# A linear-attention stage and a feed-forward stage: two programs in turn, laid out anew as one list schedule

## The chip, the cores and the metric

One core of a Trainium2 chip. The metric is the device time of one launch in microseconds; the inputs lie in device memory as float32, and the output goes back there as float32.

## What is computed

Four batches, eight heads, 768 steps, head size 48. The state of a head is a 48 x 48 matrix that decays row by row with w; the output of all heads, 384 numbers per token, goes through a multiplicative feed-forward part of 3072 tokens and width 1024.

```python
state = np.zeros((B, H, D, D))
for t in range(S):
    kt, vt, rt, wt = (k[:, :, t], v[:, :, t], r[:, :, t], w[:, :, t])
    cur = np.einsum('bhd,bhe->bhde', u[None] * kt, vt)
    y[:, :, t] = np.einsum('bhd,bhde->bhe', rt, state + cur)
    state = wt[:, :, :, None] * state + np.einsum('bhd,bhe->bhde', kt, vt)
x = y.transpose(0, 2, 1, 3).reshape(B * S, H * D)
h = (x @ w1) * (x @ w2) @ w3
out = h @ w_out
```

## The kernel before

The recurrence is done in chunks of 128 steps. Within a chunk, cumulative sums of log w (a matmul with a triangle of ones, `LT_incl` and `LT_strict`, L129 and L132) give the factors exp(-sum) for k and exp(sum) for r; a masked product of the two, times v, gives the part from inside the chunk, r times the state that the chunk began with gives the rest, and the state is carried on by k'v and the chunk's total decay (`pc_all`, L139).

Four things happen one after the other. First all constants and the four weights are set up; the weights go out on POOL's queue ahead of anything else (L84 to L87), cast to bfloat16 on the way. Then, two batches at a time (`bg`), a batch's whole r, k and v are loaded on POOL's queue (L113 to L115, pieces of 48 numbers, 6144 of them per load) and w on SP's (L116). For each batch a preparation runs over all its six chunks: the logarithm (L119), the sums, the exponentials (L130, L133), the scaled k and r (`Kt`, `Rt`, L131, L134), and the diagonal term r.(u k) v (L143 to L149). After it the chunks go by in order, the two batches in turn (L159): eight transposes of k, a copy from PSUM (`trsb`), eight of r, a copy (L166 to L171); eight products of r with the state (L178); the scores of four heads, mask, product with v, twice (L184 to L191); y goes to memory in bfloat16 (L196); eight products k'v and three small steps for the new state (L202 to L208). A head has 48 partitions in all of these.

When all of y is in memory, three transposing loads bring it back with the model dimension on partitions (L216). The feed-forward part goes by blocks of 512 tokens: eight times three matmuls each for a and b (L225, L228), ACT copies a, DVE multiplies by b (L232, L233); 64 matmuls with w3 (L239) and eight copies (L242); 32 with w_out (L247), four copies (L251) and four stores (L252).

The order on every engine is the program order. A tile framework puts the semaphores in and rotates the buffers of each pool.

Of the kernel before, what the change touches and what calls it, by code (L numbers as in the profile page):

```python
# [14 lines left out]
def kernel(
# [14 lines left out]

# [27 lines left out]
    LT_strict = consts.tile([C, C], BF)
    nc.gpsimd.memset(LT_strict, 1.0)
    nc.gpsimd.affine_select(LT_strict, LT_strict, compare_op=Alu.is_gt, fill=0.0,  # L60
                            base=0, channel_multiplier=-1, pattern=[[1, C]])

    mask_tiled = consts.tile([C, H, C], BF)
    nc.gpsimd.memset(mask_tiled, 1.0)
    nc.gpsimd.affine_select(mask_tiled, mask_tiled, compare_op=Alu.is_gt, fill=0.0,
                            base=0, channel_multiplier=-1, pattern=[[0, H], [1, C]])

    ones_c = consts.tile([C, 1], BF)
    nc.gpsimd.memset(ones_c, 1.0)

    I128 = consts.tile([C, C], BF)
    nc.gpsimd.memset(I128, 0.0)
    nc.gpsimd.affine_select(I128, I128, compare_op=Alu.not_equal, fill=1.0,
                            base=0, channel_multiplier=1, pattern=[[-1, C]])

    u_bc = consts.tile([C, H, D], F32)
    nc.sync.dma_start(u_bc, u.partition_broadcast(C))

    wpool = ctx.enter_context(tc.tile_pool(name="moe_w", bufs=1))
    w1_bf = wpool.tile([P, DI, DFF], BF)  # L80
    w2_bf = wpool.tile([P, DI, DFF], BF)
# [201 lines left out]
```

## Time and profile before

| | us |
|---|---|
| median of 3 runs (lowest, highest) | 418.54 (418.28, 418.82) |
| span of the profiled execution | 417.6 |
| PE busy | 315.4 |
| DVE busy | 175.6 |
| ACT busy | 154.9 |
| POOL busy | 33.4 |

The profile is of one execution, and it states its span, from the first to the last instruction; its whole time is not stated apart. The median of the runs is 0.9 us above that span, so the profiled execution is taken as one of them, and 0.9 us lie around the span. PE is TensorE, DVE VectorE, ACT ScalarE, POOL GpSimd, SP the queue that issues transfers. Busy PE time is pipelined and counts a matmul from its first to its last cycle, so matmuls overlap in it. The granted clock is given as a share of 2.4 GHz; 0.5 is 1.2 GHz.

### The profile page before, as it was taken

Reading aid. Unit: us, or ns where it says so; the run is one execution under the profiler, and the core shown is the slowest. Engines: PE = TensorE matmul, PEld = TensorE weight load, DVE = VectorE, ACT = ScalarE, POOL = GpSimd, SP = SyncE. Lnnn points to the kernel's source line nnn. Section 1 sums busy time; section 2 is a strip of 40 time slices with the busy share of each in tenths; the row PEclk is TensorE's granted clock in tenths of the full one; section 3 lists DMA queues with packets and bytes.
Section 4 is the critical chain, followed back from the end, with each engine's and each line's share of the span. In section 5 each row is a group of like instructions: output and inputs, shape, how many; then the busy total and the mean of one; then the engine's idle time right before and its main releaser. Section 6 shows DMA issues by size and latency. Waiting matters only on the chain.

```text
span 417.6 us, 5433 instructions
## 1 busy us (share of the span) xinstructions
PE 315.4 (76%) x2256; PEld 177.6 (43%) x2256; DVE 175.6 (42%) x264; ACT 154.9 (37%) x232; POOL 33.4 (8%) x29
## 2 busy tenths in 40 slices
PE   0301034677999747399992699999999999999996
PEld 0201021445777614177771244544544445445443
DVE  1000069795656899975573140330420411402502
ACT  1503033777465336345540133243232332331431
POOL 9100043412000400000000000000000000000000
PEclk9999999985555555655555599999999999999999
DMA  8999999979300980000004700200200201101002
GB/s 157 225 227 215 164 108 129 90 49 111 44 19 26 93 44 2 0 30 21 20 28 98 149 0 2 75 0 2 76 2 0 76 2 38 39 0 57 21 0 75
DMA packets 99400, 26.23 MB, mean 63 GB/s; under 512 B 84144, under 2 KB 97584, under 8 KB 99376
## 3 DMA queue, kind: packets, MB, share of 16 engines
q0 software_dynamic: 76800, 11.54, 40.4%
q1 hardware_dynamic: 22576, 14.36, 13.7%
q8 instruction: 17, 0.28, 0.3%
q14 instruction: 7, 0.06, 0.0%
HBM read 27.98 MB, written 7.08 MB: 84 GB/s over the span
## 4 chain that ended last, share of the span: by engine, by line
PE 63%; DVE 12%; issue 12%; ACT 4%; DMA 4%; POOL 3%; SPq 2%; ACTq 0%; POOLq 0%
PE h_ps L239 20%; PE a_ps L225 8%; PE o_ps L247 7%; PE b_ps L228 7%; PE Mps L184 5%; PE ktrps L166 4%; PE rtrps L170 4%; PE Yps L191 3%; DVE y_diag L149 2%; DMA v_bf<-in_v_dram 2%; DVE d_all L147 2%; DVE uk L146 2%; SPq L216 2%; PE Yps L178 2%; DVE Rt_bf L134 1%
## 5 line engine op out<-in xcount | busy, mean ns | idle before, releaser
L239 PE MATMUL h_ps<-abT,w_bf 128*128 128x512 bf16 x384 | 83.9, 379 | 0.0
L225 PE MATMUL a_ps<-xT,w_bf 128*128 128x512 bf16 x144 | 56.4, 396 | 11.7 <-DMA xT<-y_dram 11.7
L239 PEld LDWEIGHTS <-w_bf 128*128 128x128 bf16 x384 | 37.6, 98 | 45.3
L228 PE MATMUL b_ps<-xT,w_bf 128*128 128x512 bf16 x144 | 56.0, 393 | 0.0
L232 ACT COPY a_sb<-a_ps 128x512 f32<-128x512 f32 x48 | 28.1, 586 | 73.6 <-PE a_ps L225 72.2
L251 DVE COPY o_sb<-o_ps 128x384 f32<-128x384 f32 x24 | 13.4, 557 | 97.5 <-PE o_ps L247 97.5
L233 DVE TENSOR_TENSOR abT<-a_sb,b_ps 128x512 bf16<-128x512 f32 x48 | 33.0, 688 | 47.8 <-ACT a_sb L232 45.9
L242 ACT CAST hT<-h_ps 128x512 bf16<-128x512 f32 x48 | 28.1, 586 | 56.0 <-PE h_ps L239 56.0
L166 PE MATMUL ktrps<-I,Kt_bf 128*48 128x128 bf16 x192 | 30.3, 300 | 23.2 <-DVE Kt_bf L131 22.8
L167 ACT COPY trsb<-ktrps 48x1024 bf16<-48x1024 bf16 x24 | 24.1, 1005 | 38.4 <-PE Yps L178 36.9
L134 DVE TENSOR_TENSOR Rt_bf<-r_bf,Et 128x384 bf16<-128x384 bf16 x24 | 13.1, 546 | 54.9 <-DMA r_bf<-in_r_dram 50.8
L166 PEld LDWEIGHTS <-Kt_bf 128*48 128x48 bf16 x192 | 18.0, 139 | 33.9 <-DVE Kt_bf L131 23.0
L247 PE MATMUL o_ps<-wo_bf,hT 128*128 128x384 bf16 x192 | 32.2, 326 | 0.0
L186 DVE TENSOR_TENSOR Mbf<-Mps,mask_tiled 128x512 bf16<-128x512 f32 x48 | 30.7, 675 | 0.0
L170 PE MATMUL rtrps<-I,Rt_bf 128*48 128x128 bf16 x192 | 28.4, 304 | 2.3 <-ACT trsb L171 1.3
L129 PE MATMUL csp<-lw_bf,LT_incl 128*128 128x384 bf16 x24 | 11.0, 460 | 23.3 <-ACT lw_bf L119 12.8
L184 PE MATMUL Mps<-trsb 48*128 48x128 bf16 x192 | 28.6, 303 | 0.0
L195 DVE TENSOR_TENSOR y_c<-Yps,y_diag 128x384 bf16<-128x384 f32 x24 | 13.4, 557 | 31.2 <-PE Yps L191 31.2
L225 PEld LDWEIGHTS <-w_bf 128*128 128x128 bf16 x144 | 14.6, 101 | 27.6 <-issue 12.1
L171 ACT COPY trsb<-rtrps 48x1024 bf16<-48x1024 bf16 x24 | 24.1, 1005 | 2.1 <-PE rtrps L170 2.1
L130 ACT ACTIVATE NEt<-csp 128x384 f32<-128x384 f32 x24 | 11.7, 489 | 35.0 <-DVE Kt_bf L131 29.0
L247 PEld LDWEIGHTS <-hT 128*128 128x128 bf16 x192 | 18.8, 98 | 13.1
(51 smaller groups left out, 313.8 us busy)
## 6 DMA issues: line engine op xcount, KB each, us to landing
out_dram<-o_sb SPq DMA_DIRECT2D x24, 192.0 KB, 1.9
r_bf<-in_r_dram POOLq DMA_DIRECT2D x4, 576.0 KB, 10.5
k_bf<-in_k_dram POOLq DMA_DIRECT2D x4, 576.0 KB, 8.8
...
w_bf<-in_moe_w_dram POOLq DMA_DIRECT2D x2, 768.0 KB, 12.3
wo_bf<-in_moe_w_out_dram POOLq DMA_DIRECT2D x1, 768.0 KB, 32.2
```

The costliest lines, as they stand in the source:

```text
L166: nc.tensor.transpose(ktrps[:, h, :], Kt4[:, h, c, :], I128)
L167: nc.scalar.copy(trsb[:, 0], ktrps)
L170: nc.tensor.transpose(rtrps[:, h, :], Rt4[:, h, c, :], I128)
L184: nc.tensor.matmul(Mps[:, hi * C:(hi + 1) * C], lhsT=KtT[:, h, :], rhs=RtT[:, h, :], start=(hi == 0), stop=(hi == H // 2 - 1))
L186: nc.vector.tensor_mul(Mbf[:, g * (H // 2):(g + 1) * (H // 2), :], Mps.rearrange("s (h t) -> s h t", h=H // 2), mask_tiled[:, :(H // 2), :])
L225: nc.tensor.matmul(a_ps, lhsT=w1_bf[:, di, fi * P:(fi + 1) * P], rhs=xT[:, di, tb * TB:(tb + 1) * TB], start=(di == 0), stop=(di == DI - 1))
L228: nc.tensor.matmul(b_ps, lhsT=w2_bf[:, di, fi * P:(fi + 1) * P], rhs=xT[:, di, tb * TB:(tb + 1) * TB], start=(di == 0), stop=(di == DI - 1))
L232: nc.scalar.copy(a_sb, a_ps)
L233: nc.vector.tensor_mul(abT[:, fi, :], a_sb, b_ps)
L239: nc.tensor.matmul(h_ps, lhsT=w3_bf[:, fi, gi * P:(gi + 1) * P], rhs=abT[:, fi, :], start=(fi == 0), stop=(fi == FI - 1))
L242: nc.scalar.copy(hT[:, gi, :], h_ps)
L247: nc.tensor.matmul(o_ps, lhsT=hT[:, gi, ts * P:(ts + 1) * P], rhs=wo_bf[:, gi, :], start=(gi == 0), stop=(gi == FI - 1))
```

## The change

The whole kernel body is replaced. Operations are no longer issued where they are written. Each is entered into a list with its engine, a duration, what it reads and writes, a key (`prio`) and, where it needs them, PSUM banks; `schedule` then plays the list against those durations, an engine at a time taking the ready operation with the smallest key, and the program is issued in that order. A key is 100 per unit plus a small number, plus a constant of its kind from `RANK`. On the chip the engines run their lists in order, with semaphores between them as before.

A unit is two batches of one chunk, all sixteen heads; there are twelve, and units 2n and 2n+1 are chunk n of all four batches, 512 tokens. Each unit loads its own pieces (2048 per tensor, three buffers, four for v), so nothing is prepared ahead for a whole batch. A block is the feed-forward part of such 512 tokens and depends on the two units alone. y goes through PE transposes and one copy into `xT`; it is not stored.

w3 @ w_out is formed once on the chip (`w34_block`): eight times eight transposes of w3, a copy, eight matmuls, a copy. A block then has no w3 step.

Heads are paired: each has 64 columns, 48 of them used and the rest zero, so a transpose turns two heads at once, and a pair's scores are two products on partitions 0 to 63 and 64 to 127. The state of a pair is a 96 x 96 product of which the two diagonal parts are used (`Sbd`). The exclusive sum goes: r is multiplied by 1/w first (`RW`) and by the inclusive factor then. ruk, dv and the two state products are made on POOL, which had only constants and issues before. The copies out of PSUM are of 768, 1024 and 2048 elements. Of the diff, the parts with the keys and the operations (the removed body is the function printed above; only the lines of its that have no counterpart are repeated):

```diff
@@ -27,229 +185,424 @@
...
-        for bg in range(B // BG):
...
-                    nc.sync.dma_start(
-                        y_dram[b * S + c * C: b * S + (c + 1) * C, :].rearrange("t (h e) -> t h e", h=H),
-                        y_c)
...
-            nc.sync.dma_start_transpose(xT[:, di, :], y_dram[:, di * P:(di + 1) * P])
...
-                    nc.tensor.matmul(h_ps, lhsT=w3_bf[:, fi, gi * P:(gi + 1) * P],
-                                     rhs=abT[:, fi, :],
-                                     start=(fi == 0), stop=(fi == FI - 1))
...
+RANK = {
+    "I": -514.6, "KRT": 192.9, "KRk": 141.3, "KRr": 32.3, "LT": 346.9, "M": -298.0, "S": 275.9, "Sbd": 218.0,
+    "T": 19.3, "a": 0.7, "a_sb": 30.9, "abT": 45.1, "b": 1.1, "cs": -292.1, "dg": 759.1, "dv": -593.8,
+    "e": -725.8, "iw": 315.4, "kin": 76.5, "kv": -112.1, "ln": 105.7, "m": -532.2, "mask": -702.5,
+    "ne": 35.0, "o": 585.9, "ones": 266.0, "osb": 287.5, "pads": 788.5, "pc": -715.7, "rin": 68.6,
+    "rk": 96.2, "ruk": -33.8, "rw": 700.7, "state": 148.5, "store": -729.5, "table": -999.7, "tr": -53.7,
...
+WEIGHTS_AT = {
+    "w1": 9.47, "w2": 28.57, "w3a": 0.47, "w3b": 1.91, "wo": 1.05,
+}
...
+        kind = name.rstrip("_0123456789")
+        o = Op(eng, dur, fn, tuple(r), tuple(w), prio + RANK.get(kind, 0.0), self.LAT[eng], dma, kind, len(self.ops))
...
+                best = None
+                for o in pool:
+                    if ready_at[o] > t or (best is not None and (o.prio, o.seq) >= (best.prio, best.seq)):
+                        continue
+                    if any(self.psum[k]["at"] is None and place(self.psum[k]) is None for k in o.tiles):
+                        continue
+                    best = o
...
+    NI, NS = 3, 2
+    rin, kin, vin = (many(n, [C, BH, D], BF, x) for n, x in ((NI, "rin"), (NI, "kin"), (NI + 1, "vin")))
...
+    op("POOL", 300, c_lt, w=["LT"], prio=-42, name="LT")
...
+        ap = ROW[src][p * NB:(p + 1) * NB, :, c * C:(c + 1) * C, :].rearrange("b h t d -> t (b h) d")
+        e = nc.gpsimd if eng == "POOL" else nc.sync
+        op(eng, dur, lambda: e.dma_start(dst, ap), w=[key], prio=prio, dma=BH * C * (0.8 if eng == "POOL" else 0.85))
...
+    def wload(dst, src, key, prio, nbytes):
+        op("POOL", 950, lambda: nc.gpsimd.dma_start(dst, src), w=[key], prio=prio, dma=nbytes / 381.0)
...
+        load("SP", win[i], f"win{i}", "w", t, pr, 60)
+        load("POOL", kin[i], f"kin{i}", "k", t, pr + 1, 1350)
+        load("POOL", rin[i], f"rin{i}", "r", t, pr + 2, 1350)
+        load("POOL", vin[j], f"vin{j}", "v", t, pr + 3, 1350)
...
+    def w34_block(fi):
+        pr = 250 + fi * 12
...
+                nc.tensor.transpose(o[:, gi, :], w3_bf[:, fi, gi * P:(gi + 1) * P], I128)
...
+                nc.tensor.matmul(o[:, :DM], lhsT=w3T[fi % 2][:, gi, :], rhs=wo_bf[:, gi, :],
...
+        pr = t * 100.0
...
+        op("ACT", act(BH * D), lambda: nc.scalar.activation(LW[:, :, :D], ww, Act.Ln),
...
+                nc.tensor.matmul(o[:, b, :DM], lhsT=LT, rhs=LW[:, b * H:(b + 1) * H, :D], start=True, stop=True)
...
+                                     lhsT=LW[:, b * H + 2 * q:b * H + 2 * q + 2, :].rearrange("t h d -> t (h d)"),
...
+        op("PE", mm(384, 384, *[1] * BH), cs, r=[f"lw{s}", "LT", "ones"], w=[CS], prio=pr)
...
+        op("ACT", act(BH * D), lambda: nc.scalar.activation(IW, LW[:, :, :D], Act.Exp, scale=-1.0),
...
+        op("DVE", dve(BH * D, 2), lambda: nc.vector.tensor_mul(RW, rr, IW), r=[f"iw{s}", kr], w=[f"rw{s}"], prio=pr + 1)
...
+            nc.scalar.activation(N_.rearrange("t (b h) d -> t b (h d)", b=NB), o[:, :, :DM], Act.Exp, scale=-1.0)
...
+        op("DVE", dve(BH * D, 2), lambda: nc.vector.tensor_mul(KRs[:, 0, :, :D], kk, N_),
...
+        op("DVE", dve(BH * D, 2), lambda: nc.vector.tensor_mul(KRs[:, 1, :, :D], RW, E_),
...
+        op("DVE", dve(BH * D, 2), lambda: nc.vector.tensor_mul(rk[s], rr, kk), r=[kr, kk_], w=[f"rk{s}"], prio=pr + 8)
...
+            nc.gpsimd.tensor_mul(ruk[s].rearrange("t (b h) d -> t b h d", b=NB),
...
+        op("POOL", pool(BH * D), ruk_, r=[f"rk{s}", "u"], w=[f"ruk{s}"], prio=pr + 8)
+        op("DVE", dve(BH * D), lambda: nc.vector.reduce_sum(dg[s], ruk[s], axis=AX.X), r=[f"ruk{s}"], w=[f"dg{s}"], prio=pr + 9)
+        op("POOL", pool(BH * D), lambda: nc.gpsimd.tensor_mul(dv[s], vv, dg[s][:, :, None].to_broadcast([C, BH, D])),
...
+                        nc.tensor.transpose(o[:, b, q, :], KRs[:, x, h:h + 2, :].rearrange("t h d -> t (h d)"), I128)
...
+            nc.scalar.copy(KRTs.rearrange("p x b q t -> p (x b q t)"), o)
...
+                        nc.tensor.matmul(o[:, e, q, :], lhsT=KRTs[a:a + PAD, 0, b, q, :],
+                                         rhs=KRTs[a:a + PAD, 1, b, q, :], start=True, stop=True)
+            op("PE", mm(*[128] * H), mmul, r=[f"KRT{s}"], w=[MM], prio=pr + 7 + b)
...
+                nc.vector.tensor_mul(Mbf[m].rearrange("s j q t -> s (j q t)"), o.rearrange("s j f -> s (j f)"),
+                                     mask.rearrange("s q t -> s (q t)"))
+            op("DVE", dve(1024), msk, r=[MM, "mask"], w=[f"M{m}"], prio=pr + 7 + b)
...
+                        nc.tensor.matmul(o[:, q * 2 * D:(q + 1) * 2 * D], lhsT=KRTs[:, 1, b, q, :],
+                                         rhs=Sbd[p][:, b, q, :], start=first, stop=False)
...
+                    nc.tensor.matmul(o[:, h * D:(h + 1) * D], lhsT=Mbf[m][:, h % 2, h // 2, :],
...
+                nc.vector.tensor_add(yb[n], banks[:, g.at(Y), :][:, :DM],
...
+                    nc.tensor.transpose(o[:, di, b * C:(b + 1) * C],
...
+            nc.scalar.copy(xT[blk % 2][:, :, p * NB * C:(p + 1) * NB * C], o[:, :DI, :])
...
+                                         lhsT=KRs[:, 0, h:h + 2, :].rearrange("t h d -> t (h d)"),
+                                         rhs=vv[:, h:h + 2, :].rearrange("t h d -> t (h d)"), start=True, stop=True)
+            op("PE", mm(*[96] * (NB * HP)), kvm, r=[f"KRk{s}", kv], w=[KV], prio=pr + 11)
...
+                nc.vector.tensor_add(Tst[p].rearrange("p b q e -> p b (q e)"), o[:, :, :DM],
...
+                    nc.gpsimd.tensor_mul(Sbd[p][a:a + D, :, :, e * D:(e + 1) * D].rearrange("p b q e -> p (b q) e"),
...
+            op("POOL", 2 * pool(384), sbd, r=[f"T{p}", f"pc{t % (2 * NP)}"], w=[f"Sbd{p}"], prio=pr + 13)
...
+                    nc.gpsimd.tensor_mul(Sst[p].rearrange("p b q e -> p (b q) e"),
...
+                op("POOL", pool(768), snew, r=[f"T{p}", f"pc{t % (2 * NP)}"], w=[f"S{p}"], prio=pr + 14)
...
+        pr = (n * NP + NP - 1 + 0.9) * 100.0
...
+                    nc.tensor.matmul(banks[:, g.at(A), :], lhsT=wt[:, di, fi * P:(fi + 1) * P], rhs=xT[x][:, di, :],
...
+            op("PE", mm(512, 512, 512), am, r=xs + ["w1", "w2"], w=[A], prio=pr + fi)
+            op("PE", mm(512, 512, 512), bm, r=xs + ["w2"], w=[Bk], prio=pr + fi + 0.5)
...
+                nc.scalar.copy(a_sb[sa], banks[:, g.at(A), :])
...
+                nc.vector.tensor_mul(abT[x][:, fi, :], a_sb[sa], banks[:, g.at(Bk), :])
+            op("DVE", dve(TB), abm, r=[Bk, f"a_sb{sa}"], w=[f"abT{x}_{fi}"], prio=pr + fi - 30)
...
+                    nc.tensor.matmul(banks[:, g.at(O), :][:, :DM], lhsT=abT[x][:, fi, tt * P:(tt + 1) * P],
+                                     rhs=w34[:, fi, :], start=(fi == 0), stop=(fi == FI - 1))
+            op("PE", mm(*[DM] * FI), om, r=[f"abT{x}_{fi}" for fi in range(FI)] + [f"w34_{fi}" for fi in range(FI)],
+               w=[O], prio=pr + 40 + tt)
...
+                (nc.scalar.copy if tt % 2 else nc.vector.tensor_copy)(osb[so], banks[:, g.at(O), :][:, :DM])
+            op("ACT" if tt % 2 else "DVE", 500, oev, r=[O], w=[f"osb{so}"], prio=pr + 10 + tt)
...
+                nc.sync.dma_start(out[row:row + C, :], osb[so])
...
+        w34_block(fi)
+    for t in range(NU):
+        loads(t)
+        unit(t)
+        if t % NP == NP - 1:
+            block(t // NP)
...
+    order = g.schedule({"f": 4, "q": 6})
+    with tc.manual_schedule():
+        for o in order:
+            o.fn()
...
```

## Rows read from the trace of the kernel before

**Rows 1.** Stretches: length, busy PE, PEld, DVE, ACT, POOL, granted clock, DMA share, GB/s.

```profile
0.00:53.20 53.20, 5.58 (x99) 4.38 (x99) 1.45 (x5) 10.65 (x10) 11.24 (x19) 1.00 1.43 196
53.20:222.00 168.80, 129.33 (x1293) 87.94 (x1293) 126.64 (x186) 87.48 (x125) 22.11 (x10) 0.62 0.75 50
...
237.40:417.60 180.20, 176.73 (x856) 84.15 (x855) 46.38 (x72) 56.26 (x96) 0.00 (x0) 0.99 0.08 27
```

**Rows 2.** The chain that ended last: start us, us, what.

```profile
11.88 41.32 issue
...
115.98 0.66 PE ktrps L166 x5
...
120.43 0.66 PE ktrps L166 x5
...
277.69 13.81 PE h_ps L239 x64
291.51 5.20 PE o_ps L247 x32
```

**Rows 3.** PE in order of time near 100 us: start, us.

```profile
100.20 0.33 PE L178 MATMUL Yps<-S_bf,trsb 48*128 48x48 bf16 x4
100.47 0.73 PE L170 MATMUL rtrps<-I,Rt_bf 128*48 128x128 bf16 x5
...
103.72 0.41 PE L166 MATMUL ktrps<-I,Kt_bf 128*48 128x128 bf16 x2
...
104.70 0.50 PE L178 MATMUL Yps<-S_bf,trsb 48*128 48x48 bf16 x8
```

**Rows 4.** Stretches around the clock's fall and rise, columns as in rows 1.

```profile
92.00:94.00 2.00, 1.79 (x27) 1.38 (x25) 1.92 (x4) 1.99 (x2) 1.65 (x1) 0.50 0.17 53
...
100.00:222.00 122.00, 103.13 (x1069) 72.53 (x1068) 89.83 (x144) 59.09 (x87) 4.42 (x2) 0.51 0.34 34
...
241.00:242.00 1.00, 1.00 (x5) 0.35 (x3) 0.00 (x0) 0.24 (x1) 0.00 (x0) 0.67 0.00 0
```

**Rows 5.** Groups of DVE and ACT by shape: busy us, mean ns, idle before, releaser.

```profile
L232 ACT COPY a_sb<-a_ps 128x512 f32<-128x512 f32 x48 | 28.1, 586 | 73.6 <-PE a_ps L225 72.2 <-DVE abT L233 1.4
L149 DVE TENSOR_TENSOR y_diag<-v_bf,d_all 128x2304 bf16<-128x2304 bf16 x4 | 10.2, 2548 | 0.0
L119 ACT ACTIVATE lw_bf<-w_f 128x2304 bf16<-128x2304 f32 x4 | 8.5, 2123 | 22.5 <-DMA w_f<-in_w_dram 22.5
```

**Rows 6.** DVE in order of time near 90 us: start, us.

```profile
89.58 0.56 DVE L131 TENSOR_TENSOR Kt_bf<-k_bf,NEt 128x384 bf16<-128x384 bf16 x1
90.05 0.68 DVE L186 TENSOR_TENSOR Mbf<-Mps,mask_tiled 128x512 bf16<-128x512 f32 x1
90.65 0.55 DVE L134 TENSOR_TENSOR Rt_bf<-r_bf,Et 128x384 bf16<-128x384 bf16 x1
```

**Rows 7.** POOL in order of time; an issue counts as its work.

```profile
1.44 0.28 POOL L60 TENSOR_SCALAR_AFFINE_SELECT LT_strict<-LT_strict 128x128 bf16<-128x128 bf16 x1
2.75 1.08 POOL L65 TENSOR_SCALAR_AFFINE_SELECT mask_tiled<-mask_tiled 128x1024 bf16<-128x1024 bf16 x1
4.91 0.77 POOL L85 DMA_DIRECT2D w_bf<-in_moe_w_dram  x1
6.58 0.88 POOL L87 DMA_DIRECT2D wo_bf<-in_moe_w_out_dram  x1
9.64 2.24 POOL L114 DMA_DIRECT2D k_bf<-in_k_dram  x1
62.10 2.22 POOL L114 DMA_DIRECT2D k_bf<-in_k_dram  x1 [3.35 <-issue]
```

**Rows 8.** DMA: GB/s in 60 to 100 us; issues, KB, us to landing.

```profile
GB/s 142 145 145 145 116 77 137 144 145 116 126 130 145 142 20 0 0 28 128 132 140 144 143 145 156 134 38 7 0 0 0 0 8 98 0 59 137 133 145 114
...
out_dram<-o_sb SPq DMA_DIRECT2D x24, 192.0 KB, 1.9
...
wo_bf<-in_moe_w_out_dram POOLq DMA_DIRECT2D x1, 768.0 KB, 32.2
```

More of the change, by code (lines that the diff above doesn't have):

```diff
@@ L33 @@
     NC = S // C
-    HC = H * NC
     DM = H * D
@@ L58 @@
[L58 to L81, printed above, removed]
@@ L210 @@
[L210 to L226 removed]
+    HP = H // 2
@@ new lines, with many @@
+    PAD = 64
+    NB = 2
+    NP = B // NB
+    NU = NC * NP
+    TB = NP * NB * C
+    BH = NB * H
+    sb = ctx.enter_context(tc.tile_pool(name="sb", bufs=1))
+    ps = ctx.enter_context(tc.tile_pool(name="ps", bufs=1, space=bass.MemoryType.PSUM))
+    def many(n, shape, dt, name):
+        return [sb.tile(shape, dt, name=f"{name}_{i}", tag=f"{name}_{i}") for i in range(n)]
+    banks = ps.tile([P, 8, 512], F32, name="banks")
+    NI, NS = 3, 2
+    rin, kin, vin = (many(n, [C, BH, D], BF, x) for n, x in ((NI, "rin"), (NI, "kin"), (NI + 1, "vin")))
@@ new lines, with mm, act, dve @@
+    op = g.op
+    def mm(*cols):
+        return sum(max(n / 2.4 + 2.5, 42.0) for n in cols)
+    def act(n):
+        return 175 + 0.835 * n
+    def dve(n, x=1):
+        return 90 + 1.05 * n / x
+    def pool(n):
+        return 200 + 2.1 * n
+    def c_first():
+        nc.scalar.preload_act_table_set("natural_log_exp_and_others")
+    op("ACT", 1300, c_first, w=["table"], prio=-10, name="table")
+    def c_lt():
+        nc.gpsimd.affine_select(LT, LT, compare_op=Alu.is_ge, fill=0.0, base=0,
+                                channel_multiplier=-1, pattern=[[1, C]])
@@ new lines, in c_pads, with c_state @@
+    def c_pads():
+        for x in lw:
+            nc.vector.memset(x[:, :, D:], 0.0)
+        for x in KR:
+            nc.vector.memset(x[:, :, :, D:], 0.0)
+    def c_state():
+        for x in Sbd + Sst:
+            nc.vector.memset(x, 0.0)
+    op("DVE", 400, c_ones, w=["ones", "LT", "I128"], prio=-10, name="ones")
+    op("POOL", 300, c_lt, w=["LT"], prio=-42, name="LT")
+    op("POOL", 300, c_id, w=["I128"], prio=-41, name="I128")
+    op("DVE", 1500, c_pads, w=[f"lw{i}" for i in range(NS)] + [f"KR{x}{i}" for i in range(NS) for x in "kr"],
+       prio=-9, name="pads")
@@ new lines, with load @@
+    op("DVE", 900, lambda: nc.vector.memset(mask, 1.0), w=["mask"], prio=-8, name="mask1")
+    op("DVE", 2500, c_state, w=[f"S{i}" for i in range(NP)] + [f"Sbd{i}" for i in range(NP)], prio=-7, name="state0")
+    op("POOL", 1100, c_mask, w=["mask"], prio=-40, name="mask")
+    op("SP", 60, lambda: nc.sync.dma_start(u_bc, u.partition_broadcast(C)), w=["u"], prio=-5.0, dma=600.0, name="u")
+    ROW = {"r": r, "k": k, "v": v, "w": w}
+    def load(eng, dst, key, src, t, prio, dur):
+        c, p = divmod(t, NP)
+        ap = ROW[src][p * NB:(p + 1) * NB, :, c * C:(c + 1) * C, :].rearrange("b h t d -> t (b h) d")
+        e = nc.gpsimd if eng == "POOL" else nc.sync
+        op(eng, dur, lambda: e.dma_start(dst, ap), w=[key], prio=prio, dma=BH * C * (0.8 if eng == "POOL" else 0.85))
@@ L244 @@
[L244 to L252 removed]
+            xs = [f"xT{x}_{p}" for p in range(NP)]
@@ L256 @@
+    for fi in range(FI):
+        w34_block(fi)
[8 more added lines that the diff above has]
+            o.fn()
 _INS = ['r', 'k', 'v', 'w', 'u', 'moe_w1', 'moe_w2', 'moe_w3', 'moe_w_out']
```

481 lines of the change are left out of this document (328 added, 153 removed).

## The prediction, before the change was run

> **What bounds the kernel now.** I read the busy time of every engine in stretches first. The kernel is two programs in turn [rows 1]: up to 53.2 us TensorE is busy for 5.6 us, from there to 222 us attention runs with its clock granted at 0.62 on the mean, 15 us pass in handing over through memory, and the feed-forward part takes 180 us with PE busy for 176.7 of them and no other engine for more than 57. Next the chain of waits in order of time [rows 2]. In the first stage nothing but loading stands in it: POOL holds v's issue for 41.3 us. In attention the pieces repeat every 4.45 us per chunk and batch. In the feed-forward part it is one engine alone: 64 matmuls of w3 in 13.81 us and 32 of w_out in 5.20, six times. So one third of the span has no PE work, one third is PE at half clock, and only the last is PE at its rate.
>
> **Prices on PE.** 13.81 us for 64 is 215.8 ns per 512 columns, 5.20 for 32 is 162.5 per 384 [rows 2]. In attention five 128-column matmuls take 0.73 us and two take 0.41, so one more costs 107 ns; eight of 48 columns take 0.50 and four 0.33, so one costs 41 [rows 3]. That is columns at 1.2 GHz, and the granted clock says so: it fell to 0.50 at 92 us [rows 4], stayed there while PE issued transposes and small products without pause, and rose between 241 and 242 us, four microseconds after products of 512 columns had begun. I take half those prices, 54 and 20 ns, at 2.4 GHz.
>
> **Feed-forward part.** (h w3) w_out becomes h (w3 w_out): 384 matmuls of 215.8 ns go, 82.9 us. In their place stand, once, 64 transposes (3.5 us) and 64 products of 384 columns (10.4). A block keeps 48 of 512 and 32 of 384 columns: 15.56 us, 93.3 for six. Together 107.2 us.
>
> **Attention.** A unit is two batches of one chunk. One cumulative sum in place of two: 2 x 162 ns; 8 decay columns at 41 (0.33 us); 16 transposes of head pairs in place of 32, 0.87; 16 score products on 64 rows each. Whether two of these on different halves of the array run beside each other no row shows: between 0.43 and 0.86 us, and I take 0.86, the price of the same product before. Then 16 products of 48 and 8 of 96 columns, 0.66; 6 transposes of y, 0.33; 8 state products, 0.34. The sum is 3.7 us at full clock and 7.0 at half. Twelve units, less what the first and the last chunk leave out, are 43.1 us. The y store and the transposing loads, the 15 us of [rows 1], go altogether. **PE in all: 150.3 us**, where the feed-forward part alone had 180 us of its stretch.
>
> **The other engines.** DVE launches follow each other by 0.47 us for 384 and 0.60 for 512 elements, 0.07 more than one element per 0.96 GHz cycle [rows 6]. So 768 cost 0.87, 1024 cost 1.14. A unit has six operations of 768, two masks of 1024 and two sums of 384: 8.5 us; a block eight of 512 and two of 384, 5.7. With 6.4 for w3 w_out and some 5 of memsets DVE has 146 us: nearly as much as PE. Three of the six are products of 16-bit tensors alone, which no row shows; 1x is the upper end, half of it the lower, and I take 1x because every row of a product here is 1x [rows 5]. The Trainium skill's page "VectorE: DVE Perf Modes" (the perf-mode tier table) gives such a product 2x from SBUF; by that DVE has 132 us and the sum on PE stays the same. ACT [rows 5]: 0.85 ns per element and 0.17 us, so 6.2 us a unit and 5.7 a block, 116 in all. It is never the end.
>
> POOL gets new work. A load of 2048 pieces costs between 0.88 and 2.24 us to issue [rows 7]; on the line from 384 rows (0.77) to 6144 pieces (2.24) it is 1.2, three per unit 3.6. Its products have no row. One input costs 0.89 ns per element (1.08 us for 1024, 0.28 for 128), so 768 cost 0.85 at least; two inputs I price at twice the rate, 1.54, since that is the dearer neighbour. Three of 768 and two of 384: 6.3 us, 9.9 with the issues, 125 for all. It has room on the mean, but it is in order: behind a wait for a load or for DVE's state sum stand the products that the next unit of the same pair needs, so Sbd late by x makes Y late by x unless PE has a block to do.
>
> DMA: r, k and v move at 145 GB/s written [rows 8], 1.4 us for a load of 0.2 MB. 36 of them take 50 us, no more than before. The weights' last piece landed at 6.6 + 32.2 = 38.8 us with w's loads beside it [rows 7, 8]. In the new list w1's key is 947 - 60 + 156 = 1043 and w2's 2953, behind the loads of the first units, so I put w2 at about 40 us, and the first block with it.
>
> **The order at the start.** POOL takes the smallest key that is ready. LT has 347 - 42 = 305; the loads of units 0 to 2 have keys up to 279 and wait for nothing. So before LT's mask stand nine loads (10.8 us), three weight loads (2.7) and the two other constants (1.4): the first cumulative sum can run at about 15.5 us. What hides that is PE's other work only, the transposes of w3, once its half has landed.
>
> **The sum along PE.** Start 15.5. Work 150.3. Clock: until 40 us PE has transposes, small products and w3 w_out in pieces, as in the stage that stayed at 0.50; 24.5 us at half rate lose 12.2. Waits in attention: a pass of 4.45 us [rows 2] held 24 x 107 and 24 x 41 ns, 3.55 us of array time, a quarter more than the work; on the ten units after 40 us that is 9.3. Waits in blocks: none before, at most the same quarter now that ACT and DVE empty the banks between units; I take 5%, 4.7. End: a copy and a product for the last pair (0.59 + 0.68), o's copy (0.56) and the last store (1.9) [rows 5, 6, 8], 3.8. Together 195.8 us of span. The 418.54 us median of the runs stands 0.9 over the profiled span of 417.6, so **197 us**.
>
> **Rivals.**
> 1. The clock stays low beside attention. The units' transposes break up the blocks, and the units run at 7.0 instead of 3.7 us: 10 x 3.3 = 33 more, **230**. For it: 122 us of small work at 0.51 [rows 4]. Against it: blocks are 60% of PE's work and their kind of product lifted the clock within about 4 us.
> 2. DVE and POOL hold each other up and DVE becomes the bound. 8.5 + 2.9 us per unit is already PE's 3.7 + 7.8. Four of DVE's products per unit read two tensors from SBUF. If each waits 1.25 us for a POOL product (between 0 and 1.54) a unit lasts 16.4 us: 16 to start, 11 x 16.4, and 13 (an estimate: its nine steps one by one at these prices) for the last unit and 16 for the last block, **225**. It decides from a wait of about 0.5 us on. Before, POOL multiplied nothing, so no row shows it or excludes it. The Trainium skill's page "SBUF — State Buffer" (Who interferes with whom) has such a rule: a VectorE instruction with two SBUF inputs contends with a GpSimd instruction that reads SBUF, one blocking the other. No run here shows that yet.
> 3. PE hardly waits: warm from the start, score pairs side by side, no loss in blocks. 195.8 - 12.2 - 5 - 4.7, **174**.
> 4. Blocks don't lie beside attention, because w2 (key 2953) goes out only after all loads, when unit 8 frees its buffers near 120 us (15.5 + 9 x 11.5): then the blocks' 93.3, the last units' 11 and some 10 of waits follow, **235**. Against it: three buffers per input leave POOL without a ready load long before.
> 5. Slower: POOL's queue stops in its loads, as v's issue did for 41.3 us [rows 2]. Now 36 loads stand in one order with the products that attention waits for. With w of stop per unit the time is 15.5 to start + 12 x (9.9 + w) + 18.5 for the last block and its stores; 418 us needs w of 22 us in every unit. Three loads of 1.4 us of transfer against a stop of 3.4 us, as a later one had [rows 7], say no; at three times 3.4 it is 275.
>
> **How the numbers follow.** Forecast 0.56, its own range 182 to 212. Clock 0.15, DVE with POOL 0.12, unhindered 0.11, late w2 0.03, POOL's queue 0.03, of which 0.02 lie above the old time and the rest anywhere below or at it. 174 to 232 reaches from the unhindered case to the clock's, whose upper half and the last two are the 2 in 10 or less that it leaves out; it also holds the unknown prices (the scores 5 us, DVE's 16-bit products 14 us on an engine that is second). A measurement of this kernel can tell 0.2%, 0.8 us, from no change. All cases but the last are faster: 0.97, 0.01, 0.02.
>
> **What the profile would show.** Right: 384 h products gone; PE's first cumulative sum near 15 us, the first block near 40; clock 0.5 before and 1.0 after; PE busy in nearly every slice from there; o's last matmul some 3 us from the end. Rival 1: 0.5 in slices of units after 40 us. Rival 2: DVE busy all along, its products waiting for POOL's, PE idle for abT and M. Rival 3: full clock before 25 us. Rival 4: a_ps beginning past 100 us. Rival 5: POOL's idle time before its loads is the longest wait. I am wrong if PE is idle for more than a quarter of the time after 40 us.

## The result, and the profile after

The changed kernel takes **220.88 us** (220.38 to 221.66, 4 runs) against 418.68 (418.28 to 419.29, 4 runs): a ratio of 0.527, interval 0.526 to 0.529. The prediction said 197 us with a range of 174 to 232. So the direction and the range held, and the point is 23.9 us too low; the forecast's own range of 182 to 212 was missed. The profiled run took 221.23 us, 219.5 of it span.

The page of the changed kernel: span, busy time, three rows of the forty slices, and the chain by engine.

```profile
span 219.5 us, 3845 instructions
...
PE 165.2 (75%) x1536; PEld 99.9 (46%) x1536; DVE 147.6 (67%) x198; ACT 108.5 (49%) x151; POOL 118.5 (54%) x100
...
PE   0060092999457998948899579988879999999993
...
DVE  7021014689378299999999999689985698543521
...
PEclk9996557699975599999999999999999999999999
...
PE 38%; DVE 33%; DMA 10%; issue 9%; POOL 6%; ACT 2%; DVEq 0%; POOLq 0%; ACTq 0%
```

PE is busy for 165.2 of 219.5 us. It is mostly idle in the first seven slices (38 us). The clock is down to 0.50 from about 18 to 42 us, but for a stretch from 32 to 35, and again from about 62 to 76; from there on it is full. In the chain (the work that ended last, followed back) DVE has 33%, in a kernel whose prediction had it second throughout. The stretches of 10 us tell where (columns as in [rows 1]).

```profile
20.00:30.00 10.00, 2.72 (x24) 1.54 (x25) 1.52 (x2) 1.67 (x5) 2.58 (x3) 0.50 1.49 155
...
60.00:70.00 10.00, 6.20 (x83) 4.76 (x82) 7.67 (x10) 4.15 (x5) 9.86 (x9) 0.63 2.12 139
70.00:80.00 10.00, 9.35 (x34) 3.93 (x34) 5.54 (x9) 4.99 (x8) 3.88 (x3) 0.68 1.28 96
80.00:90.00 10.00, 8.47 (x73) 4.83 (x71) 9.88 (x14) 6.83 (x10) 7.86 (x7) 1.00 0.94 79
90.00:100.00 10.00, 6.96 (x111) 5.08 (x110) 9.90 (x11) 6.71 (x10) 8.46 (x7) 1.00 1.22 159
...
110.00:120.00 10.00, 9.74 (x104) 6.05 (x104) 10.00 (x15) 7.04 (x10) 7.71 (x7) 1.00 1.38 72
120.00:130.00 10.00, 5.95 (x93) 4.36 (x92) 10.00 (x11) 4.69 (x7) 7.56 (x7) 1.00 0.61 67
...
190.00:200.00 10.00, 10.00 (x79) 5.69 (x78) 4.24 (x7) 3.79 (x8) 0.00 (x0) 1.00 0.16 59
```

From 80 to 130 us DVE is busy for 9.9 to 10.0 of each 10 us, while PE has between 5.9 and 9.7: in this stretch DVE is the bound. Later it is PE, with 10.0 of 10 from 190 to 200. The first cumulative sum runs at 27.28 us, where 15.5 was predicted. PE's order in time shows what precedes the first block, the block, and the end (start, us; groups overlap by their pipelined ends, so the distance of two starts is the price).

```profile
60.34 0.49 PE L502 MATMUL banks<-I,yb 128*128 128x128 bf16 x6 [2.97 <-DVE yb L491]
...
70.68 0.50 PE L502 MATMUL banks<-I,yb 128*128 128x128 bf16 x3 [0.66 <-DVE yb L491]
70.97 1.49 PE L555 MATMUL banks<-xT,w_bf 128*128 128x512 bf16 x3
72.25 1.49 PE L560 MATMUL banks<-xT,w_bf 128*128 128x512 bf16 x3
...
175.52 0.62 PE L460 MATMUL banks<-KRT 64*128 64x128 bf16 x16
...
177.85 0.40 PE L460 MATMUL banks<-KRT 64*128 64x128 bf16 x8
...
206.03 0.81 PE L560 MATMUL banks<-xT,w_bf 128*128 128x512 bf16 x3
206.67 0.81 PE L555 MATMUL banks<-xT,w_bf 128*128 128x512 bf16 x3
...
207.97 7.96 PE L579 MATMUL banks<-w,abT 128*128 128x384 bf16 x48
```

The first block begins at 70.97 us, where 40 was predicted. Its inputs are there earlier: the y of units 0 and 1, whose last transposes start at 60.34, is copied to `xT` by 61.67, and w2, issued at 39.44, lands 19.0 us later, at 58.4. But PE works in order, and unit 2's products stand ahead of the block, down to the transposes of its y at 70.68. The block's first triples follow each other by 1.28 us, at 1.2 GHz; the last ones by 0.64, at 2.4 GHz. o's last 48 products end near 215.9, 3.6 us before the end of the span (predicted 3.8).

Two more views say what lies behind these. First POOL at the start, in order of time; what stands in brackets is the idle time before the instruction and what ended it.

```profile
1.33 0.94 POOL L318 DMA_DIRECT2D w_bf<-in_moe_w_dram  x1 [0.81 <-POOLq L620]
2.26 1.17 POOL L315 DMA_DIRECT2D rin<-in_r_dram  x1
...
4.55 1.18 POOL L315 DMA_DIRECT2D kin<-in_k_dram  x1
...
5.98 0.89 POOL L318 DMA_DIRECT2D wo_bf<-in_moe_w_out_dram  x1
...
11.37 1.16 POOL L315 DMA_DIRECT2D vin<-in_v_dram  x1 [0.32 <-DMA w_bf<-in_moe_w_dram]
15.87 1.15 POOL L315 DMA_DIRECT2D rin<-in_r_dram  x1 [3.34 <-DMA rin<-in_r_dram]
20.29 1.14 POOL L315 DMA_DIRECT2D kin<-in_k_dram  x1 [3.27 <-DMA kin<-in_k_dram]
25.77 1.14 POOL L315 DMA_DIRECT2D vin<-in_v_dram  x1 [4.34 <-DMA wo_bf<-in_moe_w_out_dram]
26.92 0.30 POOL L273 TENSOR_SCALAR_AFFINE_SELECT LT<-LT 128x128 bf16<-128x128 bf16 x1
...
32.83 0.74 POOL L318 DMA_DIRECT2D w_bf<-in_moe_w_dram  x1 [1.55 <-DMA rin<-in_r_dram]
...
39.44 0.74 POOL L318 DMA_DIRECT2D w_bf<-in_moe_w_dram  x1 [2.90 <-DMA w_bf<-in_moe_w_dram]
```

From the ninth issue to the seventeenth, at 44.76, none goes out before the load issued eight before it has landed, and all but one wait for it: v at 11.37 for w3's first half, issued at 1.33, then r for the r of 2.26, k for the k of 4.55, v for w_out. That is 11.3 us of waiting ahead of LT, which is made at 26.92, and w2's issue stands behind further such waits at 39.44. All eight waits are 23.2 us.

Second, DVE's groups by shape (busy us, mean ns, idle before, releaser).

```profile
L419 DVE TENSOR_TENSOR KR<-kin,NEt 128x768 bf16<-128x768 bf16 x12 | 13.7, 1144 | 0.0
L425 DVE TENSOR_TENSOR rk<-rin,kin 128x768 f32<-128x768 bf16 x12 | 13.2, 1102 | 3.7 <-DMA kin<-in_k_dram 3.7
...
L400 DVE TENSOR_TENSOR rw<-rin,iw 128x768 bf16<-128x768 bf16 x12 | 11.6, 966 | 2.8 <-ACT iw L398 2.8
...
L421 DVE TENSOR_TENSOR KR<-rw,Et 128x768 bf16<-128x768 bf16 x12 | 7.9, 657 | 9.2 <-ACT Et L409 8.2 <-PE banks L443 0.7
```

These four products of 768 elements read two tensors from SBUF. Their shortest cases are 546, 939, 545 and 542 ns, and their means are 1144, 1102, 966 and 657. Two rows of DVE and one of POOL show a long one and what runs beside it.

```profile
61.39 0.55 DVE L419 TENSOR_TENSOR KR<-kin,NEt 128x768 bf16<-128x768 bf16 x1
...
83.58 1.79 DVE L419 TENSOR_TENSOR KR<-kin,NEt 128x768 bf16<-128x768 bf16 x1
```

```profile
83.14 1.81 POOL L428 TENSOR_TENSOR ruk<-rk,u_bc 128x768 f32<-128x768 f32 x1 [0.74 <-DVE rk L425]
```

The scaled k takes 0.55 us at 61.39 and 1.79 at 83.58, where it ends 0.4 us after a POOL product that began 0.44 us before it. Over all 48 products of the four kinds the order in time says the same: the 21 with no POOL product beside them take their shortest time within 0.02 us; of the 27 that have one beside them for a part, 18, all between 60 and 157 us, are lengthened, by 0.16 to 1.43 us.

### The profile page after: what moved, and what is told of

The parts are those of the page before. It is cut to its first block, busy times and chain, and to the rows that moved or that the text cites. A ratio compares the mean times of both kernels' runs of the same rounds, so it can differ in the third digit from the quotient of the medians.

```text
span 219.5 us, 3845 instructions
## 1 busy us (share of the span) xinstructions
PE 165.2 (75%) x1536; PEld 99.9 (46%) x1536; DVE 147.6 (67%) x198; ACT 108.5 (49%) x151; POOL 118.5 (54%) x100
## 4 chain that ended last, share of the span: by engine, by line
PE 38%; DVE 33%; DMA 10%; issue 9%; POOL 6%; ACT 2%; DVEq 0%; POOLq 0%; ACTq 0%
PE banks L560 11%; DMA vin<-in_v_dram 10%; PE banks L555 10%; DVE Mbf L466 7%; PE banks L579 7%; DVE KR L419 5%; PE banks L443 4%; DVE abT L572 3%; DVE yb L491 3%; DVE rk L425 3%; DVE dg L432 3%; DVE rw L400 3%; PE banks L366 2%; DVE Tst L527 2%; DVE osb L586 1%
## 5 line engine op out<-in xcount | busy, mean ns | idle before, releaser
L572 DVE TENSOR_TENSOR abT<-a_sb,banks 128x512 bf16<-128x512 f32 x48 | 32.5, 682 | 20.1 <-PE banks L560 12.4
L568 ACT COPY a_sb<-banks 128x512 f32<-128x512 f32 x48 | 28.1, 586 | 32.3 <-PE banks L555 32.1
L560 PE MATMUL banks<-xT,w_bf 128*128 128x512 bf16 x144 | 40.3, 389 | 2.2 <-DVE abT L572 2.2
L555 PE MATMUL banks<-xT,w_bf 128*128 128x512 bf16 x144 | 40.4, 390 | 1.0 <-DVE abT L572 0.9
L579 PE MATMUL banks<-w,abT 128*128 128x384 bf16 x192 | 34.0, 326 | 2.2 <-DVE osb L586 2.1
L466 DVE TENSOR_TENSOR Mbf<-banks,mask 128x1024 bf16<-128x1024 f32 x24 | 28.5, 1214 | 4.8 <-PE banks L460 4.8
L428 POOL TENSOR_TENSOR ruk<-rk,u_bc 128x768 f32<-128x768 f32 x12 | 22.5, 1872 | 15.7 <-DVE rk L425 15.6
L534 POOL TENSOR_TENSOR Sbd<-Tst,pc 48x384 bf16<-48x384 f32 x20 | 18.1, 906 | 18.5 <-PE banks L480 17.7
L448 ACT COPY KRT<-banks 128x2048 bf16<-128x2048 bf16 x12 | 22.3, 1867 | 8.9 <-PE banks L443 8.1
L560 PEld LDWEIGHTS <-w_bf 128*128 128x128 bf16 x144 | 14.3, 100 | 20.9 <-issue 5.5
L555 PEld LDWEIGHTS <-w_bf 128*128 128x128 bf16 x144 | 14.4, 101 | 18.4 <-issue 3.3
L433 POOL TENSOR_TENSOR dv<-vin,dg 128x768 bf16<-128x768 bf16 x12 | 19.1, 1590 | 4.9 <-issue 2.1
L425 DVE TENSOR_TENSOR rk<-rin,kin 128x768 f32<-128x768 bf16 x12 | 13.2, 1102 | 3.7 <-DMA kin<-in_k_dram 3.7
## 6 DMA issues: line engine op xcount, KB each, us to landing
win<-in_w_dram SPq DMA_DIRECT2D x12, 384.0 KB, 10.4
```

What stands on the lines that cost most here:

```text
L425: op("DVE", dve(BH * D, 2), lambda: nc.vector.tensor_mul(rk[s], rr, kk), r=[kr, kk_], w=[f"rk{s}"], prio=pr + 8)
L428: nc.gpsimd.tensor_mul(ruk[s].rearrange("t (b h) d -> t b h d", b=NB), rk[s].rearrange("t (b h) d -> t b h d", b=NB), u_bc[:, None, :, :]. ...
L433: op("POOL", pool(BH * D), lambda: nc.gpsimd.tensor_mul(dv[s], vv, dg[s][:, :, None].to_broadcast([C, BH, D])), r=[f"dg{s}", kv], w=[f"dv{ ...
L448: nc.scalar.copy(KRTs.rearrange("p x b q t -> p (x b q t)"), o)
L466: nc.vector.tensor_mul(Mbf[m].rearrange("s j q t -> s (j q t)"), o.rearrange("s j f -> s (j f)"), mask.rearrange("s q t -> s (q t)"))
L555: nc.tensor.matmul(banks[:, g.at(A), :], lhsT=wt[:, di, fi * P:(fi + 1) * P], rhs=xT[x][:, di, :], start=(di == 0), stop=(di == DI - 1))
```

## The experiments

Two theories stood after the profile. The start: POOL's order holds up LT and u*r*k, or else the loads themselves do. The middle: DVE's products wait for POOL's, and DVE bounds the stretch. All times are medians of 4 runs; the kernel before stood beside them at 418.7 to 418.9 us.

**e1_mask_first.** Only LT's place on POOL changes: `move` puts an operation right behind another one of POOL's list.

```diff
     order = g.schedule({"f": 4, "q": 6})
...
+    move("LT", "I128", "LT")
```

> One move on POOL's list: the triangle LT is made right after the identity, at about 6 us, not behind twelve issues at 26.9 us; all else stays in its place. Theory A (POOL's whole list is late, LT is one item of it): the first cumulative sum goes from 27.3 to about 15.7 us, but ruk of unit 0 still stands behind the issues at 33.6 us, DVE's list has the sum dg behind it and the scaled k behind that, so the scaled k stays at 36 us and the first block at 71: 219.5 to 221 us, no more than 1.5 us less than 220.9. Theory B (LT alone was the late start): the 11.4 us that PE waited for it come off, 209 to 211 us. Theory C (loading bounds the start whatever the order): 220 to 221 us with the cumulative sum early.

220.41 us (220.17 to 221.82). The first cumulative sum comes at 15.3 us, just where the prediction had put it, and nothing is gained: the scaled k comes at 37.57 (36.30 in the changed kernel), the first block at 71.6. DVE now waits 14.9 us for u*r*k, which stands behind the same issues.

**e2_ruk_before_issues.** Moves three issues behind the first u*r*k as well.

```diff
+    for key in ("w1", "vin3", "vin2"):
+        move(key, "ruk0")
```

> The same, and on POOL's list ruk of unit 0 goes ahead of the issues of v of units 2 and 3 and of w1, which move behind it in their order. Theory A: ruk starts at about 21.5 us, when rk is there, in place of 33.6; dg at 24 and the scaled k at 25 in place of 36.3 us; the units run some 10 us earlier and the first block starts when w2 has landed, 59 to 62 us in place of 71: 209 to 213 us. Theory C (loading bounds): units earlier but the first block at 69 us or later, 218 us or more. Theory D (from 80 us on DVE is the bound, and what is won before is lost in its queue): the first block earlier and the time still 217 us or more.

219.71 us (219.32 to 220.49). The scaled k comes at 23.98, 12 us earlier, yet the first block at 70.1. Unit 1's r landed at 33.3 us and its k at 37.5. So neither LT nor u*r*k alone holds up the start. Unit 1's k does until 37.5; from there to 70 the chain has no wait for a load in it, only steps of the units and of w3 @ w_out on PE, DVE, ACT and POOL, in the order of the lists.

**e4_pool_writes_only.** POOL's products become fills of about the same length with one-column copies that keep the dependences (those on v and u are dropped; no product of POOL waited for these in the changed kernel). The diagonal term and the carried state are left out of the result. Shown for one product:

```diff
-        op("POOL", pool(BH * D), lambda: nc.gpsimd.tensor_mul(dv[s], vv, dg[s][:, :, None].to_broadcast([C, BH, D])),
+        def dv_():
+            nc.gpsimd.tensor_copy(dv[s][:, 0, 0:1], dg[s][:, 0:1])
+            nc.gpsimd.memset(dv[s], 0.0)
+            nc.gpsimd.memset(dv[s], 0.0)
+        op("POOL", pool(BH * D), dv_,
```

> The products on POOL (ruk, dv, the two of the state) are replaced by two fills of the same tile and a copy of one column of each input, so POOL's time and its waits stay about the same but it hardly reads SBUF; the diagonal term and the state are left out of the result. Same order on every engine. Theory E (a product of DVE with two SBUF inputs waits for a POOL instruction that reads SBUF): the means of DVE's rw, scaled k, scaled r and rk fall from 966, 1144, 657 and 1102 ns to 555, 555, 555 and 945, DVE's busy time from 147.6 to 133 us, and since DVE is busy for 99 in 100 from 80 to 160 us the time falls by 8 to 14 us, to 207 to 213. Rival F (those products are long for another reason, the write side or the transfers): means above 900 for the first two, DVE above 144 us, time within 3 us of 220.9.

211.84 us (211.21 to 212.48), 9.0 less, with POOL busier than in the changed kernel (127.4 us against 118.5). DVE's groups, same columns:

```profile
L425 DVE TENSOR_TENSOR rk<-rin,kin 128x768 f32<-128x768 bf16 x12 | 11.4, 953 | 3.8 <-DMA kin<-in_k_dram 3.8
...
L421 DVE TENSOR_TENSOR KR<-rw,Et 128x768 bf16<-128x768 bf16 x12 | 6.7, 555 | 9.6 <-ACT Et L409 8.6 <-PE banks L484 0.7
L400 DVE TENSOR_TENSOR rw<-rin,iw 128x768 bf16<-128x768 bf16 x12 | 6.6, 553 | 4.1 <-ACT iw L398 2.8 <-DMA rin<-in_r_dram 1.3
L419 DVE TENSOR_TENSOR KR<-kin,NEt 128x768 bf16<-128x768 bf16 x12 | 6.6, 552 | 0.0
```

Every product falls back to its shortest time, the twenty or so that have a fill beside them too. The order is unchanged and POOL is busier than before, so what held DVE is what POOL's products do and its fills do not, that is their reading of SBUF. The gain lies in the middle: the first block comes at 73.6 us, 2.6 later than in the changed kernel, and PE's idle time from 80 to 160 us falls from 13.4 to 4.9 us.

**e5_copies_on_act.** Twelve output copies go from DVE to ACT, at the same place.

```diff
-                (nc.scalar.copy if tt % 2 else nc.vector.tensor_copy)(osb[so], banks[:, g.at(O), :][:, :DM])
+                nc.scalar.copy(osb[so], banks[:, g.at(O), :][:, :DM])
```

> The 12 copies of the output out of PSUM that DVE had are issued on ACT, at the same place of the order; ACT has 24 of them. DVE is relieved of 6.6 us, ACT gets 5.8. If DVE is the bound from 80 to 160 us, the copies of the first three blocks (six of 0.55 us) come off there, and o's banks come free without waiting for DVE's list: 2.5 to 6 us less, 215 to 218.5. If PE or the waits of the units' own chain are the bound, 220 to 222; if ACT's list is too full, above 222.

216.40 us (216.29 to 216.74), 4.5 less for 7.9 us less on DVE (139.7 busy), within the 2.5 to 6 expected if DVE is the bound in the middle; ACT is not.

**e3_loads_by_unit.** Other load keys, and the list worked out anew.

```diff
-    "w1": 9.47, "w2": 28.57, "w3a": 0.47, "w3b": 1.91, "wo": 1.05,
+    "w1": 0.89, "w2": 0.94, "w3a": 3.45, "w3b": 3.47, "wo": 3.46,
-    op("POOL", 300, c_lt, w=["LT"], prio=-42, name="LT")
+    op("POOL", 300, c_lt, w=["LT"], prio=-1242, name="LT")
```

> The list is worked out anew with the mask first on POOL and with other load keys: the loads of units 0 and 1 go out first, then w1 and w2, then unit 2's loads, and w3 and w_out last (nothing that attention needs waits behind w3 and w_out any more). Theory C (loading bounds the start): first cumulative sum at 8 to 13 us, unit 1's k landed by 22 us instead of 37 (run e2), first block at 35 to 45 us instead of 70.97. What this gives is bounded by DVE, which was busy without gaps from 80 us to 160 us: if its work starts some 25 us earlier, the time is 198 to 208 us, with DVE busy for over 72% of the span. Rival D (the middle is bound by something that the start doesn't move, such as w3 and w_out, which now arrive later and hold up w34 and with it all output products): the first block comes early and the time is still 215 us or more, with PE idle later on.

211.89 us (211.55 to 212.36), 9.0 less. The first cumulative sum comes at 6.5 us and the first block at 37.7, 33 us earlier; a quarter of that reaches the end. The time lies between the two expectations: 198 to 208 was too hopeful, and it is not 215 either. DVE is busy for 9.5 to 10.0 of each 10 us from 100 to 130, loads fill the DMA engines up to about 85 us, and from 36.8 to 68.9 us the chain is one wait for a load of k (start, us, what).

```profile
36.77 32.13 DMA kin<-in_k_dram
```

The order of the loads and the whole list change together here, so the 9.0 us is what both give; the loads' part alone was not measured.

**e6_loads_and_copies** and **e7_uk_product_16bit** add to e3 the copies of e5, and then r*k and u*r*k in bf16 with u*r*k on DVE. In both the list is worked out anew.

```diff
-    rk = many(NS, [C, BH, D], F32, "rk")
-    ruk = many(NS, [C, BH, D], F32, "ruk")
+    rk = many(NS, [C, BH, D], BF, "rk")
+    ruk = many(NS, [C, BH, D], BF, "ruk")
...
-            nc.gpsimd.tensor_mul(ruk[s].rearrange("t (b h) d -> t b h d", b=NB),
+            nc.vector.tensor_mul(ruk[s].rearrange("t (b h) d -> t b h d", b=NB),
```

> As e3_loads_by_unit, and the twelve output copies that DVE makes are given to ACT (the list plans with that). If DVE is the bound (theory E with C), it is 3 to 5 us faster than e3_loads_by_unit, as e5 was 4.5 us faster than the changed kernel, with DVE busy some 8 us less. If loading or the late w34 bounds (rival D), it is within 1 us of e3_loads_by_unit.

> As e6_loads_and_copies, and r*k and u*r*k are kept as bf16 and u*r*k is made on DVE, not POOL: POOL loses 12 products of 1.81 us (22 us busy), DVE gains 12 of 0.55 us and its r*k falls from 0.95 to 0.55 us (0.15 us per unit more in sum, 2 us). Theory E (a two-input product of DVE waits for POOL instructions that read SBUF): about 40% of POOL's reading time is gone, so 15 us of excess in DVE's durations falls to 8 to 10 us, and the time is 2 to 5 us under e6_loads_and_copies. Rival (POOL's reads hold DVE only through the three products other than u*r*k): no excess goes, DVE is 2 us busier and the time is equal or up to 2 us longer.

216.00 us (214.93 to 217.75) and 222.45 (221.81 to 222.96): 4.1 and 10.6 slower than e3, where less was expected, although DVE is busy for 143.2 and 142.1 us instead of 145.9. e7's waits of DVE between 50 and 90 us (us in total, times, longest) say what happened there.

```profile
DVE w L373 <- PE banks L368: 13.4, 2, 10.4
DVE w3T L361 <- PE banks L368: 6.8, 2, 4.9
DVE yb L493 <- POOL dv L435: 3.7, 1, 3.7
```

DVE stands in its order before the copies of w3 @ w_out for 20.2 us, and the attention work queued behind those copies stands with it. w_out's load, which holds 13% of e7's chain, had landed by 55.1 us and is not what the longest wait, 10.4 us up to 75.4, goes back to: there POOL waits 5.7 us for a load before an issue, the state product behind it ends at 71.4, ACT has waited 11.2 us for that, and the copy of w3's transposes that PE needs stands next in ACT's list.

**e8_copies_in_place** and **e9_uk_16bit_in_place** make the same two edits, but leave e3's list as it is (u is cast to bf16 once, ahead of the first product).

> As e3_loads_by_unit with its list left as it is; only the twelve output copies of DVE are made by ACT, at the same place of the list. e6, which gave the same copies to ACT and let the list be worked out anew, was 4.1 us slower than e3. Theory F (e6's loss came from the order that the list then chose, with w34 and its waits elsewhere): here, with the order kept, 207 to 210.5 us, since DVE is still busy for 9 to 10 of each 10 us from 100 to 150 us. Rival (ACT's copies hold up the blocks themselves): 214 us or more, as e6.

> As e8_copies_in_place, and r*k and u*r*k in bf16 with u*r*k on DVE, again at the same places of the list. Theory F with E: POOL about 96 us busy, DVE within 1 us of e8's busy time, means of the three other products at 0.60 to 0.85 us instead of 0.65 to 1.2, the time 1 to 5 us under e8. Rival (e7's extra 6.4 us came from the product on DVE itself): 3 us or more over e8.

209.73 us (208.70 to 210.58) and **200.69** (200.46 to 201.29). The same edit is 4.1 us slower than e3 with a new list and 2.2 faster with the old one, and the next is 21.8 us apart between the two. So theory F holds: e6 and e7 lost by the order. e9 is 9.0 under e8, where 1 to 5 was expected. e9 does the whole computation and beats both kernels: 0.479 of the time before (0.478 to 0.481). Its page:

```profile
span 198.9 us, 3840 instructions
...
PE 160.7 (81%) x1529; PEld 98.3 (49%) x1536; DVE 137.1 (69%) x199; ACT 113.1 (57%) x163; POOL 95.9 (48%) x88
...
PE   0235293759999789749998699999999999999992
...
DVE  7235786169833599998999996999975985615400
...
PEclk9999997599999999978999999999999999999999
```

POOL has 95.9 us (119.2 in e8), DVE 137.1, and the clock is down only near 35 us and, less, near 90. The means of r*w, the scaled r and the scaled k are 0.86, 0.67 and 0.62 us (1.13, 0.68, 0.74 in e8). What the four products of e8 take over their shortest times falls only from 11.7 to 8.9 us, so less waiting for POOL's reads does not explain 9.0 us. The edit also takes 23 us off POOL's list and spares u*r*k the way from DVE to POOL and back (DVE waits 4.0 us for it in e8, not at all in e9). These parts were not separated.

**e10_loads_and_writes_only** is e3 with e4's fills.

> As e3_loads_by_unit with POOL's products replaced by fills and one-column copies, as in e4 (left out: the diagonal term and the carried state). It asks whether the start (e3: 9 us) and the wait of DVE's products for POOL's reads (e4: 9 us) add up. If they do: 202 to 205 us, DVE 132 us busy, its 16-bit products at 0.55 us. If loading is what bounds e3 up to 85 us and PE after it: 206 to 211 us, with the same DVE times.

199.96 us (198.52 to 200.46): 20.9 less than the changed kernel, where the two parts alone gave 9.0 each. They add up, and 2.9 us more, below the 202 to 205 expected; where these come from was not shown.

**e11_uk_16bit_alone** is e9's edit on the changed kernel, with nothing else.

> The changed kernel, its list and loads untouched; only r*k and u*r*k are kept in bf16 and u*r*k is made by DVE at the same place of the list. Nothing is left out. Theory E (DVE's products wait for POOL's reads, and DVE bounds the stretch from 80 to 160 us): 22 us of POOL's reads go, the mean of r*w falls from 966 to under 800 ns and of the scaled k from 1144 to under 900 ns, the time is 211 to 216 us. Rival (the 9 us of e9 need the earlier loads, since here the first block at 71 us decides): 218 us or more.

211.57 us (211.05 to 212.22), 9.3 less. DVE's groups and two stretches of it:

```profile
L420 DVE TENSOR_TENSOR KR<-kin,NEt 128x768 bf16<-128x768 bf16 x12 | 8.7, 723 | 0.2 <-ACT NEt L405 0.2
L401 DVE TENSOR_TENSOR rw<-rin,iw 128x768 bf16<-128x768 bf16 x12 | 8.4, 704 | 2.8 <-ACT iw L399 2.8
```

```profile
80.00:100.00 20.00, 17.53 (x202) 11.36 (x202) 19.64 (x27) 16.65 (x24) 15.36 (x12) 1.00 0.97 130
100.00:120.00 20.00, 17.02 (x202) 11.01 (x201) 20.00 (x30) 12.32 (x16) 12.18 (x12) 1.00 1.01 70
```

The scaled k has a mean of 723 ns (1144 before), r*w 704 (966). DVE does twelve products more and is busy for 142.0 us instead of 147.6. It is still full from 80 to 120 us. The first block comes at 67.9 us, 3 earlier. PE's idle time from 80 to 160 us falls by 4.0 us, half of what e4 gives there; the rest lies in the start and in PE's busy time (161.1 us for 165.2).

## Why the prediction was right, and where it failed

**Set against its own sum.** Predicted span 195.8, measured 219.5: 23.7 us to find. PE is idle for 28.2 of the first 40 us, predicted 15.5: **12.7**. It is idle for 26.1 after that, predicted 9.3 + 4.7 + 3.8 = 17.8: **8.3**. It is busy for 165.2, predicted 150.3 + 12.2 = 162.5: **2.7**. A further 0.8 us lies outside the span (1.7 against 0.9). Of the 26.1 us, 7.8 lie between 40 and 80 us, 13.4 between 80 and 160, and 4.9 at the end. So the extra idle time lies ahead of 80 us, and the 14.0 us that the sum had for waits nearly equal the middle's 13.4, but by luck: there DVE is the bound, and no quarter on PE's own work is what PE waits for. Luck has a part in the range too: 220.9 lies outside 182 to 212, and inside 174 to 232 only because that range takes in rivals 1 and 2. Rival 1 did not come; of rival 2 the mechanism came and not the price.

**Right.** The large step: the h products are gone, PE's work is close to 150 us (165.2 less 9.8 us of clock, each stretch's busy time by what its clock lacks of 1.00, is 155.4), and the 15 us of the hand-over have gone. This is read from the two traces; no run takes a part of the change back. One reading of the kernel before is off: up to 53.2 us and from 222 to 237 are a sixth of its span, not a third; the sum does not use it. Clock: 12.2 predicted, 9.8 measured; it is up from 80 us on while units and blocks alternate, so rival 1 is wrong. It also fell a second time, at about 62 us, after PE had been idle from 57.4 to 60.3, and was back at 76, while the first block ran; no step had this. The ends match (3.6 for 3.8). POOL's prices match: an issue 1.2 (measured 1.15 to 1.20), a product of 768 elements 1.54 (shortest 1.47 for the state, 1.48 for v, 1.81 for u*r*k in f32; means 1.50, 1.59 and 1.87), 118.5 us in all for 125; ACT 108.5 for 116. PE idle after 40 us is 15%, under the quarter named.

**The score products.** Eight take 0.40 us and sixteen 0.62 in the trace, so eight more cost 0.22, 27 ns each: half the 54 of a product of 128 columns (transposes of 128 columns at full clock in the same trace: eight in 0.62 us, sixteen in 1.06), at the lower end of the bounds. The products alternate between the two halves of the array, and in the kernel before, products on 48 rows cost their full columns [rows 3], so two on different halves run beside each other. I had taken the upper end; it is worth 5 us on paper.

**Wrong: the start** ("the first cumulative sum can run at about 15.5 us", "I put w2 at about 40 us, and the first block with it"). The step counted the issues' own durations and no wait. It had a stop of POOL's queue only as rival 5, at another price. The wait for the load eight issues before made the cumulative sum 11.8 us late, but e1 shows that this alone costs nothing. The bytes came later than the step had them: the four weight tensors' 4352 KB and three units of 960 KB, 7232 KB, go out before w2 has landed, which at 145 GB/s [rows 8] is 51 us, an estimate that the prediction could have made. w2 landed at 58.4 us, unit 1's k at some 37 even in e2. And the block does not begin with w2: it also needs the y of units 0 and 1, there at 61.7 us, and stands behind unit 2 in PE's list, so it ran at 71. e3, with other loads first and a new list, begins it at 37.7 and is 9.0 us faster; how much of this is the loads and how much the list stays open.

**Wrong: the waits in attention and blocks** (9.3 and 4.7, and DVE as "an engine that is second"). DVE's total came out at 147.6 us for 146, by two errors that cancel. The products of 16-bit tensors take 0.55 us for 768 elements, not 0.87, as the lower bound had it; and they take 15 us more in sum than that (twelve times 413, 592, 102 and 149 ns over e4's means), because they wait for POOL. On the first, the Trainium skill's page "VectorE: DVE Perf Modes" (the perf-mode tier table) gives such a product of 16-bit tensors in SBUF 2x. The trace agrees, with 0.55 us; r*k, whose output is f32, takes 0.95, and 0.54 at the shortest with a 16-bit output (e11). On the second, the Trainium skill's page "SBUF — State Buffer" (Who interferes with whom) states that a VectorE instruction with two SBUF inputs contends with a GpSimd instruction that reads SBUF and not with one that only writes. The runs agree with both halves: 0.55 us beside e4's fills, up to 1.98 beside the changed kernel's products. So rival 2's mechanism was there. Its price was not: the wait is 0.31 us per product on the mean (15 us over 48), or 0.84 for the 18 that wait at all, not 1.25 for each, and its mean is below the 0.5 that I had put as the point from which it decides. It still decided the middle: 9.0 us by e4.

Both steps together are worth e10's 20.9 us in this kernel. That is not the 23.9 us found over again: in e10 DVE has 133 us, where the sum had 146. Rival 3 (unhindered, 174) came in none of the runs. w2 was 18 us late, but not for rival 4's reason, and the first block did not wait for it. Rival 5's stop was 23.2 us in all, up to 44.8 us, not 22 in every unit.

**Open.** How much of e3's 9.0 us is the loads and how much the new list was not separated. The clock has little part in it: two of the changed kernel's four runs had 0.958 and 0.966 on the mean, about what e3 has (0.950 to 0.957), and took 220.38 and 220.53 us, about 1 less than the two at 0.922. Why e6's order loses was not followed further than that the same edit in the old order does not.
